# Fourier steps with the real and imaginary halves side by side on 128 rows, fewer index steps, and another written-out order

## The chip, the cores and the metric

The kernel runs on one core of a Trainium2 chip. The metric is the device time of one execution, in microseconds. The core's engines are PE (TensorE, matmuls; PEld is its weight load), DVE (VectorE), ACT (ScalarE), POOL (GpSimd) and SP (SyncE, which here issues nearly all transfers). Each works through its own instructions in order, and they wait for one another by semaphores.

## The reference

Two branches read the same input x of 2,048 positions and 512 channels, and a gate mixes them:

```python
x = A_u
g = _sigmoid((x * gate_w).sum(-1, keepdims=True))
a = _A_ref(x, ...)      # state-space convolution
b = _B_ref(x, ...)      # linear attention, 32 heads of 16
return g * a + (1 - g) * b

# _A_ref: a filter of 2,048 taps for each channel, applied by Fourier transform
P = jnp.exp(logdA[:, :, None] * l[None, None, :])
K = jnp.einsum("dn,dnl,dn->dl", Cc, P, dB).real
Kf = rfft2(pad(K, L));  Uf = rfft2(pad(u, L))
y = irfft2(Uf * Kf)[:, :L] + u * Dskip

# _B_ref: phi = concat(softmax(p), softmax(-p)) for queries and keys
kv = jnp.einsum("bhsf,bhsd->bhfd", phi_k, v);  z = phi_k.sum over s
o = (phi_q @ kv) / (phi_q . z + 1e-6);  return o @ wo
```

## The kernel before, in words

**What is computed where.** The filter is made in 16 units of 32 channels: PE makes arguments (args), ACT takes exponentials (E, line 71) and sines (cs, line 71), DVE multiplies them to tables (A, lines 1012 to 1027, and R, lines 1036 and 1040), and PE multiplies A by R to the taps of the unit (kps, line 175), which are evicted to KD. Both the input and the filter go through a Fourier transform of 4,096 points in two steps. *Stage a* multiplies by the table W1 (line 589 for the input, line 1067 for the filter) and is evicted to XAu or XA; *stage b* (fft_stage_b, line 186) multiplies, for each of 32 residues, by a table TB and is evicted to xst or XK. The input's spectrum goes to DRAM (XUd) and comes back as XUX or XUY. Then DVE multiplies the spectra (t, line 1129), PE does the first inverse step (psz, line 1156), the result Zr goes to DRAM (Zd, line 1167) and comes back turned (ZT, line 1176), PE does the second inverse step (psy, line 1218) on top of the attention's result, DVE multiplies by the gate (ou, line 1240), and the output is written (line 1249). This is done for channels 0 to 127, 128 to 255, 256 to 383, then for units 12 and 13 (64 channels), 14 (32) and 15 (32). Unit 15 is turned on the core itself, without DRAM (pszn, psyn).

**The layout of the two Fourier steps.** Before, the 128 rows between the steps hold two groups of 64 rows for two halves of the channels; real and imaginary parts lie side by side along the row. Stage a of the input is, for a chunk, 8 matmuls of 256 columns with 64 weight columns each; stage a of the filter is 4 matmuls of 256 columns with 128 weight columns. Stage b is, for each residue, four matmuls over 64 rows: real and imaginary part times two row groups, with sine, cosine and negated sine in TB.

**What sets the order.** The program is a list of 1,070 steps. A step has a name and an engine or a choice of two: an eviction may be on ACT or DVE, other table steps on DVE or POOL. Plan.ORDER is a written-out order of all steps, Plan.SIDES the choices of engine, Plan.RINGS the choices between two PSUM pools. run() emits the steps in that order, so each engine, and SP's queue of transfers, gets its own steps in the order of the list and works them off strictly so. In this text a step is called by its name and a number that counts the steps of that name as the program adds them: zw.14 is the fifteenth write of a Zd block.

**Names that the text uses.** *First 74 us:* `first` makes the index columns (build_index_cols, lines 50 to 55); tg1 (line 250) and tg2 (line 251) make the arguments of a trigonometric table and tgs (ACT) its sines; w1 (lines 261 and 263) makes W1; tbn (line 270) the negated table; tjs (line 287) scales a table for the inverse; st1 to st3 (lines 318 to 321) split parameters into two parts, which pzw writes to DRAM (line 325) and pzr reads back; p_t (lines 359, 360), p_cn (line 426), p_dd (its negation is line 435) and others belong to the chain of the parameters, which ends with p_de; ud.0 to ud.3 are the loads of the input (UD, line 1342), four transfers each; xps turns the input for the attention. *Attention:* pk and vp (lines 699, 738) are keys and values, ek and eq exponentials on ACT, kvp their product; z1 to z5 are the norms, aw writes them to DRAM, ar reads them back spread out (ax, line 870) and em multiplies by them (Eq, line 877). *Transfers at the end:* zw (line 1167) and zr (line 1176) write and read Zd, out (line 1249) writes the output.

The step that hands a chunk of stage a to ACT or DVE is an eviction:

```python
def copy(self, o, i):
    if self.cur.at == "ACT":
        self.nc.scalar.copy(out=o, in_=i)
    else:
        self.nc.vector.tensor_copy(out=o, in_=i)
```

## Time and profile before

| what | value |
|---|---|
| median of 3 runs | 306.41 us (304.59 to 309.04) |
| profiled execution: time | 307.27 us |
| profiled execution: span | 305.4 us |
| matmuls / weight loads | 4,732 / 4,758 |
| DVE, ACT, PE, POOL busy | 256.1, 239.2, 219.2, 48.2 us |
| granted TensorE clock, mean | 0.92 |
| moved by transfers | 35.95 MB |

A group line of the profile reads: source line, engine, operation, output tile <- input tiles, shapes, number of instructions | busy us, mean ns of one | idle time of the engine just before, and what ended it. A timeline line reads: start, length, engine, line, operation, shapes, number merged, and in brackets idle time before with what ended it. A line of the chain of waits reads: start, length, what. SPq is SP's queue: the length of a transfer's line there is the time until SP had issued it, not until it landed.

### The profile page before, as it was taken

Reading aid. Unit: us, or ns where it says so; the run is one execution under the profiler, and the core shown is the slowest. Engines: PE = TensorE matmul, PEld = TensorE weight load, DVE = VectorE, ACT = ScalarE, POOL = GpSimd, SP = SyncE. Lnnn points to the kernel's source line nnn. Section 1 sums busy time; section 2 is a strip of 40 time slices with the busy share of each in tenths; the row PEclk is TensorE's granted clock in tenths of the full one; section 3 lists DMA queues with packets and bytes.
Section 4 is the critical chain, followed back from the end, with each engine's and each line's share of the span. In section 5 each row is a group of like instructions: output and inputs, shape, how many; then the busy total and the mean of one; then the engine's idle time right before and its main releaser. Section 6 shows DMA issues by size and latency. Waiting matters only on the chain.

```text
span 305.4 us, 10610 instructions
## 1 busy us (share of the span) xinstructions
PE 219.2 (72%) x4732; PEld 140.7 (46%) x4758; DVE 256.1 (84%) x339; ACT 239.2 (78%) x328; POOL 48.2 (16%) x53
## 2 busy tenths in 40 slices
...
GB/s 151 250 200 83 60 0 2 104 105 82 126 49 161 210 3 54 156 2 119 67 242 20 137 12 172 77 361 149 75 39 81 301 110 147 228 111 108 175 63 113
DMA packets 62620, 35.95 MB, mean 118 GB/s; under 512 B 46192, under 2 KB 56048, under 8 KB 62576
## 3 DMA queue, kind: packets, MB, share of 16 engines
...
q10 hardware_dynamic: 4224, 0.92, 1.9%
...
## 4 chain that ended last, share of the span: by engine, by line
DVE 25%; PE 24%; ACT 18%; DMA 12%; issue 6%; SPq 1%; ACTq 0%; DVEq 0%
DMA ax<-apd 5%; DMA Zd<-Zr 4%; PE pk L699 4%; PE vp L738 4%; PE kps L175 4%; PE psB L186 3%; DVE R L1040 2%; ACT cs L71 2%; ACT E L71 2%; DVE A L1012 2%; ACT XK L142 2%; PE psz L1156 2%; ACT XA L142 2%; DMA ZT<-Zd 2%; DVE Dtab L360 2%
## 5 line engine op out<-in xcount | busy, mean ns | idle before, releaser
L175 PE MATMUL kps<-R,A 128*32 128x64 bf16 x1472 | 26.0, 227 | 12.8 <-issue 6.4
L71 ACT ACTIVATE E<-args 128x1024 bf16<-128x1024 f32 x32 | 32.7, 1058 | 0.1
L175 PEld LDWEIGHTS <-A 128*32 128x32 bf16 x1472 | 24.0, 152 | 17.5 <-issue 9.0
L71 ACT ACTIVATE cs<-args 128x1024 bf16<-128x1024 f32 x32 | 30.6, 1063 | 0.2 <-DVE R L1040 0.2
L186 PEld LDWEIGHTS <-TB 64*128 64x128 bf16 x1024 | 20.9, 98 | 15.3 <-issue 11.9
L589 PE MATMUL psA<-W,UD 128*64 128x256 bf16 x128 | 14.0, 352 | 11.4 <-DVE XAu L144 4.8
L1012 DVE TENSOR_TENSOR A<-Ctab,Dtab 128x2048 bf16<-128x2048 bf16 x16 | 19.6, 1222 | 2.7 <-PE kps L175 2.7
L1036 DVE TENSOR_TENSOR R<-E,cs 128x2048 bf16<-128x2048 bf16 x16 | 19.5, 1220 | 1.3 <-ACT cs L71 1.3
L142 ACT CAST XK<-psB 128x1024 bf16<-128x1024 f32 x15 | 15.5, 1043 | 6.4 <-PE psB L186 5.2
L508 PE MATMUL xps<-ident,UD 128*128 128x128 bf16 x64 | 8.2, 309 | 16.2 <-DMA UD<-in_A_u_dram 9.2
L714 DVE TENSOR_REDUCE Zk<-Ek 128x64 f32<-128x1024 bf16 x16 | 18.7, 1212 | 1.3 <-ACT Ek L71 1.3
L1040 DVE TENSOR_TENSOR R<-E,cs 128x2048 bf16<-128x2048 bf16 x16 | 19.5, 1220 | 0.0
L589 PEld LDWEIGHTS <-UD 128*64 128x64 bf16 x128 | 10.6, 200 | 15.7 <-issue 9.7
L71 ACT ACTIVATE Eq<-pq 128x512 bf16<-128x512 f32 x32 | 17.1, 619 | 0.4 <-PE pq L811 0.4
...
L71 ACT ACTIVATE Ek<-pk 128x512 bf16<-128x512 f32 x32 | 16.8, 604 | 0.6 <-PE pk L699 0.4
L811 PE MATMUL pq<-xT,Wqp 128*128 128x512 bf16 x64 | 17.0, 408 | 0.0
L1156 PE MATMUL psz<-t,TI 128*128 128x512 bf16 x51 | 16.4, 415 | 0.7 <-issue 0.2
L186 PE MATMUL psB<-XAu,TB 64*128 64x128 bf16 x256 | 11.8, 247 | 6.6 <-DVE xst L144 3.2
L142 ACT CAST XA<-psA 128x1024 bf16<-128x1024 f32 x14 | 14.4, 1058 | 2.8 <-PE psA L1067 2.8
L910 PE MATMUL bps<-wo 128*128 128x512 bf16 x58 | 16.2, 380 | 0.5 <-DVE wo L144 0.2
L699 PE MATMUL pk<-WW,xT 128*128 128x512 bf16 x61 | 16.2, 399 | 0.3 <-issue 0.2
...
## 6 DMA issues: line engine op xcount, KB each, us to landing
...
```

Of the source, the lines that this page charges most:

```text
L71: return self.nc.scalar.activation(**kw)
L142: self.nc.scalar.copy(out=o, in_=i)
L175: nc.tensor.matmul(kps[32 * dj:32 * dj + 32, g4, e, :], lhsT=A[:, ka, :, :, d].rearrange("p a b -> p (a b)"), rhs=R[:, kr, d, :], start=(i ...
L186: nc.tensor.matmul(ps[:, e, sl, :], lhsT=fc.TB[rows, r, 1 - ri:3 - ri, :].rearrange("p a b -> p (a b)"), rhs=XA[rows, r, ri, :], start=(ri ...
L589: nc.tensor.matmul(box.ps[64 * e:64 * e + 64, i, :], lhsT=g.UD[:, :, 64 * h + 32 * e + 4 * g4 + i], rhs=W1, start=True, stop=True, tile_po ...
L699: nc.tensor.matmul(box.ps[:], lhsT=xT[:, st, kt, :], rhs=g.WW[:, kt, :], start=(kt == 0), stop=(kt == 3))
L714: nc.vector.tensor_reduce(out=z, in_=e, axis=mybir.AxisListType.X, op=ALU.add)
L811: nc.tensor.matmul(box.ps[:], lhsT=g.Wqp[:, kt, 128 * m:128 * m + 128], rhs=xT[:, 4 * b:4 * b + 4, kt, :], start=(kt == 0), stop=(kt == 3))
L1012: nc.vector.tensor_tensor(out=c.A[:, 0:2].rearrange("p o a b c -> p (o a) b c"), in0=g.C[:, 0:2, :, d0:d0 + 32].rearrange("p o a c -> p (o ...
L1036: nc.vector.tensor_tensor(out=c.R[:, :, :, 32:64], in0=t.E[:].rearrange("p e x t -> p (e x) t")[:, :, 32:64].unsqueeze(1).to_broadcast([12 ...
L1040: nc.vector.tensor_tensor(out=c.R[:, :, :, 0:32], in0=t.E[:].rearrange("p e x t -> p (e x) t")[:, :, 0:32].unsqueeze(1).to_broadcast([128, ...
L1156: nc.tensor.matmul(box.ps[:, nr * hb:nr * hb + nr, :], lhsT=fc.TI[:, k].rearrange("p t h a -> p (t h a)"), rhs=box.t[:, k, rt:rt + nr, :], ...
```

## The change

The rows between the two Fourier steps now hold the real part in rows 0 to 63 and the imaginary part in rows 64 to 127 of the same channels.

- W1 is kept as two halves. Stage a (new function fft_stage_a) does two matmuls of 128 columns for each 64 weight columns, one into the upper and one into the lower rows: 16 per chunk, for the input and for the filter.
- TB holds two tables instead of three, already different in the upper and the lower rows (new step `two` makes their two offsets), so the negated table (tbn, two steps) is not made. Stage b is one matmul over 128 rows for each residue, with all columns: a quarter as many matmuls.
- The channel order within a unit (kgen_chunk) and the access patterns of the evictions XAu, XU, XA and XK follow the new layout. An eviction still moves 1,024 elements of each row.
- build_index_cols makes eight index columns in one tile and casts them with one instruction instead of eight. One iota of 128 is kept and used in w1, sel0 and at0, where four others were made.
- The list has 1,069 steps, and ORDER, SIDES and RINGS are new.

Counted from the list: matmuls of stage a of the input 128 to 256, of the filter 64 to 256; of stage b 1,024 to 256.

Steps by engine, before and after: DVE 263 and 274, ACT 274 and 271, POOL 29 and 20, PE 274 each. From POOL to DVE go three of the ten tg1 (net), the second st1, st2 and st3, one tjs, two p_cn and p_t.14; from DVE to POOL go w1, at3 and p_t.9.

SP's queue, first part. Before: ud.0 wqk ld ud.1 ud.3 ud.2 wv wsm pzw.1 pzw.0 pzr.0 pzr.1. After: wsm wqk ud.1 wv ld ud.0 ud.3 pzw.0 ud.2 pzw.1 pzr.0 pzr.1.

SP's queue, last part. Before: zw.11 xur.7 zr.4 zr.5 zw.12 zw.13 zr.6 zr.7 out.0 zw.14 zr.8 zr.9 out.2 out.1 out.3. After: zw.11 xur.7 zr.4 zr.5 out.0 zw.12 zw.13 zr.6 zr.7 zw.14 zr.8 zr.9 out.1 out.2 out.3. out.0 follows ou.3, and zr.8 and zr.9 read what zw.14 wrote.

PE, last part. Before: psB32.0 psy128.4 psy128.5 kps.8 psz.14 psA.15 psB32.1 psy64.0 pszn.0 psyn32.0 psy32.0. After: psy128.4 psy128.5 psB32.0 kps.8 psA.15 psz.14 psB32.1 psy64.0 pszn.0 psyn32.0 psy32.0. Zr.14 is on DVE before and on ACT, behind XA.15, after.

The first norms. Before, on ACT: z3.0, four cs, z5.0; after: z3.0 eq.7 z5.0, four cs. On DVE, from z4.0 to em.0, before: Rl.0 Rh.1 Rl.1 A1.1 A2.1 A3.1 KD.0 A1.2 A2.2 z2.1; after: A2.0 A3.0 Rh.0 Rl.0 Rh.1 Rl.1.

```diff
 def build_index_cols(nc, pool):
     idx_i = pool.tile([128, 1], I32, name="idx_i")
     nc.gpsimd.iota(idx_i[:], pattern=[[0, 1]], base=0, channel_multiplier=1)
-    cols = {}
-
-    def mk(name, shift, mask):
-        t = pool.tile([128, 1], I32, name=f"ii_{name}")
+    want = (("p", 0, 127), ("p31", 0, 31), ("p63", 0, 63), ("h16", 4, 7), ("h2", 4, 1), ("s5", 5, 3), ("b5", 5, 1), ("b6", 6, 1))
+    t = pool.tile([128, len(want)], I32, name="ii")
+    f = pool.tile([128, len(want)], F32, name="if")
+    for k, (name, shift, mask) in enumerate(want):
         if shift:
-            nc.vector.tensor_scalar(out=t[:], in0=idx_i[:], scalar1=shift, scalar2=mask,
+            nc.vector.tensor_scalar(out=t[:, k:k + 1], in0=idx_i[:], scalar1=shift, scalar2=mask,
                                     op0=ALU.arith_shift_right, op1=ALU.bitwise_and)
         else:
-            nc.vector.tensor_single_scalar(out=t[:], in_=idx_i[:], scalar=mask, op=ALU.bitwise_and)
-        f = pool.tile([128, 1], F32, name=f"if_{name}")
-        nc.vector.tensor_copy(out=f[:], in_=t[:])
-        cols[name] = f[:, 0:1]
-    mk("p", 0, 127); mk("p31", 0, 31); mk("p63", 0, 63)
-    mk("h16", 4, 7); mk("h2", 4, 1); mk("s5", 5, 3); mk("b5", 5, 1); mk("b6", 6, 1)
-    return cols
+            nc.vector.tensor_single_scalar(out=t[:, k:k + 1], in_=idx_i[:], scalar=mask, op=ALU.bitwise_and)
+    nc.vector.tensor_copy(out=f[:], in_=t[:])
+    return {name: f[:, k:k + 1] for k, (name, _, _) in enumerate(want)}
...
-    ORDER = ("01020H0R0a0b0d030V0e000S040M0m0n0c050706080o0T0W191a0U0N0O0Z0X0f15160g0P0h0I111b0B0C0-0J17180K0L340_1c0Q1d1p0i100D091e12"
...
+    ORDER = ("0H1o0R0S0T0a0W0b0c01020405030y0z0A0X070I080B0d0M0J06000Y0K1L0N0C0O0e0p0q1s090P0Z140U0f110D3j3l180r39191a0L0V1O0Q15160-1d"
...
-                    d = 16 * e + 4 * dj + g4
+                    d = 8 * g4 + 4 * e + dj
                     nc.tensor.matmul(kps[32 * dj:32 * dj + 32, g4, e, :], lhsT=A[:, ka, :, :, d].rearrange("p a b -> p (a b)"),
                                      rhs=R[:, kr, d, :], start=(i == 0), stop=(i == len(terms) - 1), tile_position=(0, 32 * dj), skip_group_check=True)
 
 
+def fft_stage_a(nc, fc, ps, lhsT):
+
+    for ri in range(2):
+        nc.tensor.matmul(ps[64 * ri:64 * ri + 64], lhsT=lhsT, rhs=fc.W1[:, ri].rearrange("p r d -> p (r d)"), start=True, stop=True, tile_position=(0, 64 * ri))
+
+
 def fft_stage_b(nc, fc, ps, XA, r0, ns):
 
     for sl in range(ns):
-        r = r0 + sl
-        for ri in range(2):
-            for e in range(2):
-                rows = slice(64 * e, 64 * e + 64)
-                nc.tensor.matmul(ps[:, e, sl, :], lhsT=fc.TB[rows, r, 1 - ri:3 - ri, :].rearrange("p a b -> p (a b)"), rhs=XA[rows, r, ri, :],
-                                 start=(ri == 0), stop=(ri == 1), tile_position=(64 * e, 0), skip_group_check=True)
+        nc.tensor.matmul(ps[:, sl, :], lhsT=fc.TB[:, r0 + sl].rearrange("p a b -> p (a b)"), rhs=XA[:, r0 + sl], start=True, stop=True)
...
-        F.w1 = g.ctmp.tile([128, 32, 2], BF16, name="w1")
+        F.w1 = g.ctmp.tile([128, 2, 32], BF16, name="w1")
...
     def w1(e):
-        c4 = F.one[:, 0:4]
-        iota_f(nc, c4, [[1, 4]])
-        e.tensor_scalar(out=F.one[:, 4:8], in0=c4, scalar1=g.icol["s5"], scalar2=None, op0=ALU.is_equal)
+        e.tensor_scalar(out=F.one[:, 4:8], in0=g.c128[:, 0:4], scalar1=g.icol["s5"], scalar2=None, op0=ALU.is_equal)
         for dj in range(4):
             e.tensor_scalar(out=fc.W1[:, :, :, dj], in0=F.w1[:], scalar1=F.one[:, 4 + dj:5 + dj], scalar2=None, op0=ALU.mult)
     E("w1", w1, r="ic w10 w11", w="W1 one")
+
+    def two(e):
+        e.tensor_scalar(out=F.two[:, 0:1], in0=g.icol["b6"], scalar1=SIN - COS, scalar2=COS, op0=ALU.mult, op1=ALU.add)
+        e.tensor_scalar(out=F.two[:, 1:2], in0=g.icol["b6"], scalar1=COS - MSIN, scalar2=MSIN, op0=ALU.mult, op1=ALU.add)
+    E("two", two, r="ic", w="two")
     tb = lambda i, hf: fc.TB[:, 16 * hf:16 * hf + 16, i, :]
     for hf in range(2):
         c, kc = iot([[2, 16], [128, 64]], 1 + 32 * hf, 1024)
-        for i, o in ((0, SIN), (1, COS)):
-            trig(lambda i=i, hf=hf: tb(i, hf), 1024, p63, lambda o=o: o, c, kc, f"TB{i}{hf}")
-        E("tbn", lambda e, hf=hf: e.tensor_scalar(out=tb(2, hf), in0=tb(0, hf), scalar1=-1.0, scalar2=None, op0=ALU.mult), r=f"TB0{hf}", w=f"TB2{hf}")
+        for i in range(2):
+            trig(lambda i=i, hf=hf: tb(i, hf), 1024, p63, lambda i=i: F.two[:, i:i + 1], c, kc, f"TB{i}{hf}", None, "two ")
...
-                    X.t = g.xau.tile([128, 32, 2, 128], BF16, name="XAu", tag="XAu")
-                box.ps = psum([128, 4, 256], "psA")
-                for i in range(4):
-                    for e in range(2):
-                        nc.tensor.matmul(box.ps[64 * e:64 * e + 64, i, :], lhsT=g.UD[:, :, 64 * h + 32 * e + 4 * g4 + i],
-                                         rhs=W1, start=True, stop=True, tile_position=(0, 64 * e))
+                    X.t = g.xau.tile([128, 32, 4, 64], BF16, name="XAu", tag="XAu")
+                box.ps = psum([128, 8, 128], "psA")
+                for i in range(8):
+                    fft_stage_a(nc, fc, box.ps[:, i, :], g.UD[:, :, 64 * h + 8 * g4 + i])
 
             def ea(g4=g4, box=box, X=X):
-                i = box.ps[:].rearrange("p g (x d) -> p x d g", d=4)
+                i = box.ps[:].rearrange("p c (r d) -> p r d c", d=4)
                 box.ps = None
-                return X.t[:].rearrange("p r i (d g) -> p (r i) d g", d=4)[:, :, :, 4 * g4:4 * g4 + 4], i
+                return X.t[:, :, :, 8 * g4:8 * g4 + 8], i
...
-                box.ps = psum([128, 2, 4, 128], "psB")
-                fft_stage_b(nc, fc, box.ps, X.t, r0, 4)
+                box.ps = psum([128, 4, 256], "psB")
+                fft_stage_b(nc, fc, box.ps, X.t[:].rearrange("p r d c -> p r (d c)"), r0, 4)
                 if r0 == 28:
                     X.t = None
 
             def eb(r0=r0, box=box):
-                i = box.ps[:].rearrange("p e s (d g) -> p s d e g", d=4)
+                i = box.ps[:].rearrange("p s (d c) -> p d s c", d=4)
                 box.ps = None
-                return box.s[:].rearrange("p d s (e g) -> p s d e g", e=2)[:, r0 % 8:r0 % 8 + 4], i
+                return box.s[:, :, r0 % 8:r0 % 8 + 4, :], i
...
-                    XA.t = g.xap[XA.slot].tile([128, 32, 2, XA.nd // 2], BF16, name="XA", tag="XA")
-                box.ps = psum([128, 4, 256], "psA")
-                for i in range(4):
-                    nc.tensor.matmul(box.ps[:, i, :], lhsT=K.KD[:, cc, i, :], rhs=W1, start=True, stop=True)
+                    XA.t = g.xap[XA.slot].tile([128, 32, XA.nd], BF16, name="XA", tag="XA")
+                box.ps = psum([128, 8, 128], "psA")
+                for i in range(8):
+                    fft_stage_a(nc, fc, box.ps[:, i, :], K.KD[:, cc, i // 2, 64 * (i % 2):64 * (i % 2) + 64])
                 if cc == nu - 1:
                     K.KD = None
 
             def ex(cc=cc, box=box):
                 slot = (0 if new else 2) + cc
-                i = box.ps[:].rearrange("p g (x d) -> p x d g", d=4)
+                i = box.ps[:].rearrange("p c (r d) -> p r c d", d=4)
                 box.ps = None
-                return XA.t[:].rearrange("p r i (c d g) -> p (r i) c d g", d=4, g=4)[:, :, slot, :, :], i
+                return XA.t[:, :, 32 * slot:32 * slot + 32].rearrange("p r (c d) -> p r c d", d=4), i
...
-                box.ps = psum([128, 2, ns, ng], "psB")
+                box.ps = psum([128, ns, nd], "psB")
                 fft_stage_b(nc, fc, box.ps, XA.t, r0, ns)
                 if end:
                     XA.t = None
 
             def xk(box=box):
                 box.XK = g.fpool.tile([128, ns, nd], BF16, name="XK", tag="XK", bufs=g.P.k["XK"])
-                o = box.XK[:].rearrange("p s (c e x) -> p (s c) e x", e=2, x=16)
-                i = box.ps[:].rearrange("p e s (c x) -> p (s c) e x", x=16)
+                i = box.ps[:]
                 box.ps = None
-                return o, i
+                return box.XK[:], i
...
-        fc.W1 = persist.tile([128, 32, 2, 4], BF16, name="W1")
-        fc.TB = persist.tile([128, 32, 3, 64], BF16, name="TB")
+        fc.W1 = persist.tile([128, 2, 32, 4], BF16, name="W1")
+        fc.TB = persist.tile([128, 32, 2, 64], BF16, name="TB")
```

67 lines of the change are left out of this document (31 added, 36 removed).

## The prediction

> **What bounds the kernel now.** I read the page's totals first, then the busy time of each engine by stage, then the timeline of the first and the last stage, and the chain of waits where a stage is tight.
>
> ```profile
> span 305.4 us, 10610 instructions
> PE 219.2 (72%) x4732; PEld 140.7 (46%) x4758; DVE 256.1 (84%) x339; ACT 239.2 (78%) x328; POOL 48.2 (16%) x53
> ```
>
> The windows below are start:end, length, then busy time and instructions of PE, PEld, DVE, ACT and POOL, the granted clock, DMA share and GB/s.
>
> ```profile
> 0.00:74.00 74.00, 38.84 (x435) 31.07 (x437) 67.78 (x125) 57.28 (x70) 40.51 (x45) 0.91 0.51 99
> 74.00:113.00 39.00, 37.42 (x667) 19.84 (x673) 33.83 (x39) 34.29 (x64) 7.70 (x9) 1.00 0.44 124
> 113.00:148.00 35.00, 27.00 (x464) 13.41 (x464) 29.70 (x48) 34.35 (x57) 0.00 (x0) 0.90 0.25 79
> 148.00:248.00 100.00, 81.74 (x1871) 52.36 (x1883) 95.80 (x103) 94.09 (x121) 0.00 (x0) 0.98 0.43 131
> 248.00:306.00 58.00, 34.24 (x1305) 24.03 (x1306) 29.00 (x28) 19.23 (x21) 0.00 (x0) 0.78 0.73 137
> ```
>
> No engine bounds the whole. The tables and the parameter chain (to 74 us) are DVE's, 67.78 of 74; the keys (to 113) are PE's, 37.42 of 39; then ACT's (34.35 of 35), then DVE and ACT together; after 248 no engine is full, and the time is that of transfers and of the order in which SP issues them. So I price the change stage by stage.
>
> **The first 74 us.** The change drops seven casts, the two negated tables (tbn) and four iotas, and it moves steps between DVE and POOL.
>
> ```profile
> 1.20 0.15 DVE L53 TENSOR_SCALAR ii_p<-idx_i 128x1 int32<-128x1 int32 x1 [1.20 <-POOL mpi L224]
> ...
> 3.12 0.15 DVE L55 CAST if_b<-ii_b 128x1 f32<-128x1 int32 x1
> ...
> 3.42 0.74 DVE L250 TENSOR_SCALAR tgv<-tgc,if_p 128x1024 int32<-128x1024 f32 x1
> ...
> 9.58 0.99 DVE L261 TENSOR_SCALAR one<-one,if_s 128x4 f32<-128x4 f32 x1
> ...
> 10.68 0.79 DVE L263 TENSOR_SCALAR W<-w,one 128x64 bf16<-128x64 bf16 x4
> ...
> 29.22 1.50 DVE L359 TENSOR_TENSOR pt<-pt,pt 128x512 f32<-128x512 f32 x1
> ...
> 32.54 0.69 DVE L359 TENSOR_TENSOR pt<-pt,pt 128x512 f32<-128x512 f32 x1 [0.23 <-ACT pt L71]
> ...
> 33.15 1.22 DVE L144 CAST XAu<-psA 128x1024 bf16<-128x1024 f32 x1
> ```
>
> ```profile
> 57.21 2.74 POOL L359 TENSOR_TENSOR pb<-pb,pb 128x1024 f32<-128x1024 f32 x1 [20.51 <-DVE pb L409]
> ...
> 57.76 2.89 DVE L435 TENSOR_SCALAR trg<-trg 128x1024 bf16<-128x1024 bf16 x1
> ...
> 70.89 0.43 DVE L435 TENSOR_SCALAR trg<-trg 128x1024 bf16<-128x1024 bf16 x1
> ```
>
> ```profile
> L270 POOL TENSOR_SCALAR TB<-TB 128x1024 bf16<-128x1024 bf16 x2 | 6.3, 3144 | 0.1
> ```
>
> ```profile
> 57.76 2.90 DVE trg L435
> ```
>
> DVE's own tally: the sixteen tiny index steps take 3.27 - 1.20 = 2.07 us; nine of them and two for "two" remain, 11/16 of it, 1.42: -0.65. w1 goes to POOL: -(0.99 + 0.79) = -1.78. Up to the end of the parameter chain the new sides give DVE two 1,024-wide evictions fewer: -2.44; ACT, 57.28 of 74 busy, takes them. Onto DVE come two long tg1 (2 x 0.74), the second st1 to st3 (at most 3 x 0.69), tjs and two p_cn (3 x 0.43, by the like operation at 70.89), and p_t.14 for p_t.9 (a 1,024-wide pass, at most 1.38, for a 512-wide one, 0.69): +5.5. Net +0.7 us.
>
> Against that stands what POOL does to DVE. The same operation took 2.89 us while POOL's 2.74 us pass ran and 0.43 without; another pair is 1.50 against 0.69. Those two rows alone hold 2.46 + 0.81 = 3.3 us, and p_t.14, both p_cn, both tbn (6.3 us of POOL) and a tjs leave POOL. The relief lies between nothing (POOL keeps two p_t and gets w1) and twice the two rows, 6.6; I take 4.7, nearer the upper end, because the chain of waits, whose line for it stands last of the fences on POOL, has the 2.9 us on it. The term: 0.7 - 4.7 = **-4 us, between -6 and +1**. The Trainium skill, SBUF — State Buffer, section on who interferes with whom, says that VectorE in its fast modes and GpSimd hold a shared port pair as an exclusive lock, the loser blocking for the whole instruction; the trace agrees, 2.89 being about POOL's 2.74 and not a little over 0.43. The sum would be the same without that rule.
>
> The negated table itself is read only by stage b of the input, which follows all evictions of stage a; that it goes saves POOL's time and nothing on PE's path.
>
> **Stages a and b on PE.**
>
> ```profile
> 59.20 1.74 PE L660 MATMUL gps<-gw,xT 128*128 128x1 bf16 x64
> ```
>
> ```profile
> 79.08 0.65 PE psA L589 x8
> ...
> 86.52 0.55 PE psB L186 x16
> ...
> 217.28 0.59 PE psB L186 x32
> ...
> 221.34 1.97 PE kps L175 x128
> ...
> 236.63 1.05 PE psA L1067 x8
> ...
> 280.97 1.79 PE psB L186 x128
> ```
>
> Stage a of the input: 8 passes of 256 columns per chunk become 16 of 128, equal streaming, twice the weight loads. Bounds: 0.55, sixteen load-and-pass pairs of 128 columns as psB has them, to 0.65 plus eight pairs at twice the kps pace (1.97/128 = 15 ns for 32 weight columns, 31 for 64) = 0.90. I take 0.65, as streaming is unchanged and eight loads fit in it now. Only the 8 chunks of the keys' stage are on the path: 0, between -0.8 and +2. Stage b of the input: 4 pairs with 256 columns, half of 1.05, against 0.55: nothing. Stage a of the filter: four pairs (0.53) become sixteen (0.55 to 0.90), four chunks of it after 248: +0.4, at most +1.5. Stage b at 128 channels: eight pairs of 128 columns, between 0.53 and 0.59: nothing. At 32 and 64 channels 128 short passes take 1.79; 32 full-height loads with short passes, at the pace of L660 (1.74/64 = 27 ns), take 0.87: -0.9 in each of three blocks after 248, -2.7. The evictions keep their 1,024 elements; I price them alike.
>
> What speaks against stage a: the Trainium skill, TensorEngine Tiling, Gotcha 2, says that column tiling excludes fast weight load, and the filter's stage a now tiles columns. TensorE: Matmul & The Clock Gate, section on LDWEIGHTS, prices a load at columns / 1.2 ns, 53 ns for 64 columns, an estimate of 0.85 us per chunk if loads alone pace it; the sum would then be about 300.3. No run here shows such loads paced alone.
>
> **The middle.**
>
> ```profile
> 127.53 7.44 ACT cs L71 x8
> ...
> 140.37 7.33 DMA ax<-apd
> 147.72 1.23 DVE Eq L877
> ```
>
> Before, z5.0 stands behind the first cs group on ACT, and the ax transfer then keeps DVE waiting. After, z5.0, aw.0 and ar.0 precede the group, so the 7.33 lie beside the 7.44. DVE was idle only 35 - 29.70 = 5.3 us in that window, ACT was full, and the new order puts six passes between z4.0 and em.0 on DVE (A2.0, A3.0 and four R; 7.4 us at the 1.23 of the Eq row), while the ax transfer alone takes 7.33 and its write and issue come before it, so em.0 still waits, with A1.1 and all behind it queued on DVE, and kps.1 on PE behind those. I take **-1 us, between -3 and +3**.
>
> **The end.**
>
> ```profile
> 262.08 4.97 SPq L1176 DMA_DIRECT2D ZT<-Zd  x2
> ...
> 273.27 1.24 SPq L1167 DMA_DIRECT2D Zd<-Zr  x2
> ...
> 279.47 1.23 DVE L144 CAST Zr<-psz 128x1024 bf16<-128x1024 f32 x1 [2.41 <-PE psz L1156]
> ...
> 280.00 4.98 SPq L1249 DMA_DIRECT2D out_dram<-xT  x4
> ...
> 285.03 1.32 SPq L1167 DMA_DIRECT2D Zd<-Zr  x1
> ...
> 293.48 9.02 SPq L1249 DMA_DIRECT2D out_dram<-xT  x10
> ```
>
> The last far block is ready at 279.47 + 1.23 = 280.70, but its write zw.14 leaves at 285.03: SP was issuing out.0 for 4.98 us. Everything after (zr.8, zr.9, psy32, out.3) hangs on it. After the change out.0 is issued behind zr.5, in SP's gap from 267.05 to 273.27, which holds 6.2 us; it is then ahead of zw.12, which waits only if zr.5 comes late. So 4.33 us go. Given back: psz.14 now follows psA.15 on PE and Zr.14 follows XA.15 on ACT; psA is 0.53, and the eviction pushes Zr.14 by up to another 0.7: +1.2. Of the -2.7 and +0.4 of PE I count -1, because DVE's passes before t32.0 (Rh, Rl, A1, A2, A3) and SP's issues are next. The term: -4.33 + 1.2 - 1 = **-4 us, between -7 and -1**. The final out queue, 9.02 us, keeps its length and shifts with zw.14.
>
> **Sum.** -4 + 0 - 1 - 4 = -9 us on the profiled execution, 307.27 (its span and 1.87 around it), which is 0.86 above the median of 306.41. From the median: **297.4 us**. The lower ends add to -6 - 1 - 3 - 7 = -17, the upper to +1 + 2 + 3 - 1 = +5.
>
> **Rivals.**
>
> ```profile
> 8.15 10.10 SPq L1342 DMA_DIRECT2D UD<-in_A_u_dram  x12
> ...
> 24.78 2.72 SPq L325 DMA_DIRECT2D pz<-pt  x4
> ...
> 33.46 2.09 PE L589 MATMUL psA<-W,UD 128*64 128x256 bf16 x16 [2.89 <-ACT xT L142]
> ```
>
> *The input comes late.* All of UD is issued by 18.25 now; in the new order ud.2 stands on SP behind pzw.0, which waits for st3.0. Now the pz writes go at 24.78; behind half of 2.72 and four UD issues (4 x 0.84 = 3.4) the last quarter would be issued at 29.5, and stage a could lose the start's -4 altogether: 301.4. For it: SP issues in order. Against it: the second stage-a chunk ran at 33.46 anyhow, and st3.0 comes earlier with a lighter DVE. Chance 0.17.
>
> *out.0 is only moved.* If zr.5 or ou.3 are late, out.0's 4.98 lands on zw.12 and zw.13, and zw.14 still leaves near 285: the end gives -1, not -4: 300.4 to 302. Chance 0.10.
>
> *Slower: weight loads of stage a stand bare.*
>
> ```profile
> L589 PEld LDWEIGHTS <-UD 128*64 128x64 bf16 x128 | 10.6, 200 | 15.7 <-issue 9.7
> ```
>
> A load is recorded at 200 ns. Sixteen of them end to end are 3.2 us a chunk instead of 0.65, +2.55 on the 12 chunks on the path (8 in the keys' stage, 4 at the end): +31, 328 us. To come out slower by 2% the change must lose 15 us against my sum, 1.26 us a chunk, so the point is 1.9 us a chunk, 119 ns a pair. Against: eight pairs run in 0.65 now, 81 ns each; at that pace sixteen take 1.3, +0.65 x 12 = +7.8, 305, which is still no change. Chance 0.09.
>
> **Chances and range.** 2%, about what a measurement of this kernel can tell from no change, is 6.1 us: below 300.3 or above 312.5. My forecast has 0.60, in its own range of 291 to 303, nine tenths of it below 300.3; the two rivals inside 2% have 0.27, stage a 0.09, and 0.04 is for both savings failing (306). Faster 0.55, no change 0.36, slower 0.09. The range 290 to 307 leaves out the slower rival and about 0.07 below.
>
> **What would show it.** Right: tgv, TJ and trg on DVE near their shorter times; the first cs group after z5.0; the last Zd write leaving within 1 us of its Zr, with out.0 before the two ahead of it; psB blocks at 32 channels under 1 us; the end of the parameter chain near 70 us instead of 74 and of the keys near 109 instead of 113. Wrong: stage-a chunks above 0.9 us; DVE stretched as before beside POOL; psAu waiting for UD; SP holding zw.12 or zw.14 behind out.0; the window 148 to 248 longer than 100 us for the same work.

## The result, and the profile after

The changed kernel takes 296.98 us (median of 4, 295.95 to 302.3) against 306.74 for the kernel before (median of 4, 304.59 to 309.04): a ratio of 0.967, 95% interval 0.958 to 0.976. The prediction was 297.4. Medians and ranges are of all runs, while ratios leave out disturbed ones, among them the first profiled execution after the change (302.3 us) and the profiled one of a_contig (293.15 us). Every line of "after" below is therefore from a later execution of the changed kernel (`after_again`), 297.03 us with a span of 294.5.

The first two lines of its page, and its count of the queue that carries instructions (transfers, MB, share of 16 engines):

```profile
span 294.5 us, 9724 instructions
PE 224.7 (76%) x4310; PEld 147.5 (50%) x4310; DVE 254.7 (86%) x336; ACT 238.4 (81%) x325; POOL 29.8 (10%) x48
...
q8 instruction: 33, 0.54, 0.8%
```

PE is busier than before (224.7 against 219.2 us) with fewer instructions, POOL is much lighter (29.8 against 48.2), DVE and ACT carry the same. So the time did not come from less work on PE, DVE or ACT. To see where it came from I cut both spans at the same events: the first exponential of the keys, the last matmul of kvp, the end of the second gate step ou.1, and the end. The kernel before (start:end, length, then busy us of PE, PEld, DVE, ACT, POOL, granted clock, DMA share, GB/s):

```profile
0.00:74.80 74.80, 39.24 (x438) 31.27 (x441) 68.58 (x126) 58.07 (x71) 41.22 (x46) 0.91 0.51 99
74.80:119.80 45.00, 43.76 (x815) 22.95 (x825) 38.99 (x45) 40.27 (x76) 6.98 (x8) 1.00 0.37 104
119.80:241.10 121.30, 96.83 (x2012) 58.89 (x2021) 112.93 (x136) 115.95 (x157) 0.00 (x0) 0.96 0.40 121
241.10:305.40 64.30, 39.40 (x1488) 27.60 (x1483) 35.61 (x36) 24.95 (x27) 0.00 (x0) 0.81 0.71 141
```

The changed kernel, cut at the same events:

```profile
0.00:70.60 70.60, 41.53 (x413) 33.45 (x415) 64.69 (x118) 59.63 (x72) 29.84 (x48) 0.76 0.55 115
70.60:118.00 47.40, 47.24 (x786) 27.68 (x785) 39.78 (x48) 39.50 (x74) 0.00 (x0) 1.00 0.32 96
118.00:236.10 118.10, 98.41 (x1928) 60.71 (x1928) 113.25 (x136) 115.47 (x155) 0.00 (x0) 0.99 0.42 124
236.10:294.50 58.40, 37.56 (x1188) 25.66 (x1187) 37.00 (x37) 23.80 (x26) 0.00 (x0) 0.83 0.74 146
```

Start -4.2, keys' stage +2.4, middle -3.2, end -5.9: together -10.9. The prediction had -4, 0, -1 and -4. The sum was close, but two of its terms were too small a gain and one hid a loss. In the keys' stage PE is busy 47.24 of 47.40 us: a full PE, and 3.5 us more of it than before.

Next come rows that answer to those shown of before. First, DVE in the start (timeline):

```profile
15.22 0.88 DVE L249 TENSOR_SCALAR tgv<-tgc,one 128x1024 int32<-128x1024 f32 x1 [1.07 <-POOL tgc L39]
...
16.83 0.62 DVE L288 TENSOR_SCALAR TJ<-tj 128x1024 bf16<-128x1024 bf16 x1
...
18.66 0.43 DVE L288 TENSOR_SCALAR TJ<-tj 128x1024 bf16<-128x1024 bf16 x1 [0.62 <-ACT tj L67]
...
32.32 3.95 DVE L394 SCALAR_TENSOR_TENSOR pb<-pt,pt 128x256 f32<-128x256 f32 x8
...
54.49 0.43 DVE L436 TENSOR_SCALAR trg<-trg 128x1024 bf16<-128x1024 bf16 x1
...
66.21 0.43 DVE L436 TENSOR_SCALAR trg<-trg 128x1024 bf16<-128x1024 bf16 x1
```

The negation of trg that had taken 2.89 us now takes 0.43 both times. The chain of the parameters (its last p_de) ends at 68.8 instead of 73.4.

Then PE, in the keys' stage and behind it. The first row is two chunks of the input's stage a, the second one chunk, the third two chunks of the filter's stage a, the last a block of stage b at 32 channels:

```profile
68.84 2.51 PE L178 MATMUL psA<-W,UD 128*64 128x128 bf16 x32 [0.66 <-ACT xst L138]
71.52 1.35 PE L178 MATMUL psA<-W,UD 128*64 128x128 bf16 x16 [0.16 <-DVE XAu L140]
...
252.45 1.08 PE L178 MATMUL psA<-W,KD 128*64 128x128 bf16 x32
...
274.74 0.95 PE L184 MATMUL psB<-XA,TB 128*128 128x32 bf16 x32
```

A chunk of the input costs 1.35 us, 84 ns a pair of load and pass (1.26 where two follow each other); the filter's 0.54, 34 ns a pair. In the same 64-column form they differ by a factor of 2.5. Stage b at 32 channels has gone from 1.79 to 0.95.

Last the end, ACT and SP:

```profile
256.65 5.77 SPq L1240 DMA_DIRECT2D out_dram<-xT  x4
266.17 2.03 SPq L1158 DMA_DIRECT2D Zd<-Zr  x2
...
274.80 1.01 ACT L138 CAST Zr<-psz 128x1024 bf16<-128x1024 f32 x1
...
275.84 0.33 SPq L1158 DMA_DIRECT2D Zd<-Zr  x1
...
282.02 10.08 SPq L1240 DMA_DIRECT2D out_dram<-xT  x10
```

out.0 is issued by 262.42, zw.12 leaves at 266.17 unhindered, and zw.14 leaves 0.03 us after its eviction, where it had waited 4.33.

### The profile page after: what moved, and what is told of

Same layout as the page of the kernel before. It is cut to its first block, busy times and chain, and to the rows that moved or that the text cites. A ratio compares the mean times of both kernels' runs of the same rounds, so it can differ in the third digit from the quotient of the medians.

```text
span 299.6 us, 9699 instructions
## 1 busy us (share of the span) xinstructions
PE 221.8 (74%) x4285; PEld 146.4 (49%) x4310; DVE 255.4 (85%) x336; ACT 238.4 (80%) x325; POOL 29.8 (10%) x48
## 4 chain that ended last, share of the span: by engine, by line
PE 34%; ACT 30%; DVE 13%; DMA 11%; issue 8%; SPq 1%; ACTq 0%; DVEq 0%
ACT cs L67 7%; PE kps L171 5%; PE pk L692 5%; PE vp L731 5%; ACT E L67 5%; PE psA L178 5%; PE psz L1147 4%; PE psB L184 3%; DMA wqk<-in_B_wqkv_dram 3%; ACT L64 3%; ACT Zr L138 3%; DMA ax<-apd 2%; DMA ZT<-Zd 2%; ACT Eq L67 2%; ACT xT L138 2%
## 5 line engine op out<-in xcount | busy, mean ns | idle before, releaser
L171 PE MATMUL kps<-R,A 128*32 128x64 bf16 x1472 | 27.6, 231 | 9.3 <-issue 7.2
L171 PEld LDWEIGHTS <-A 128*32 128x32 bf16 x1472 | 25.7, 160 | 13.3 <-issue 9.6
L178 PE MATMUL psA<-W,UD 128*64 128x128 bf16 x256 | 21.1, 316 | 8.8 <-DVE pt L361 3.8
L178 PEld LDWEIGHTS <-UD 128*64 128x64 bf16 x256 | 20.1, 246 | 11.0 <-issue 10.8
L184 PEld LDWEIGHTS <-TB 128*128 128x128 bf16 x256 | 15.6, 100 | 12.8 <-issue 6.8
L1147 PE MATMUL psz<-t,TI 128*128 128x512 bf16 x52 | 17.0, 430 | 1.8 <-ACT XK L138 0.7
L138 ACT CAST Zr<-psz 128x1024 bf16<-128x1024 f32 x14 | 14.3, 1032 | 3.1 <-PE psz L1147 2.4
L1120 DVE TENSOR_TENSOR t<-XUX,XK 128x1024 bf16<-128x1024 bf16 (+1 forms) x22 | 15.6, 732 | 0.8 <-ACT XK L138 0.8
L731 PE MATMUL vp<-WW,xT 128*128 128x512 bf16 x57 | 15.7, 396 | 0.3
L138 ACT CAST KD<-kps 128x1024 bf16<-128x1024 f32 (+1 forms) x7 | 6.3, 899 | 11.4 <-PE kps L171 11.4
```

The costliest lines, as they stand in the source:

```text
L171: nc.tensor.matmul(kps[32 * dj:32 * dj + 32, g4, e, :], lhsT=A[:, ka, :, :, d].rearrange("p a b -> p (a b)"), rhs=R[:, kr, d, :], start=(i ...
L178: nc.tensor.matmul(ps[64 * ri:64 * ri + 64], lhsT=lhsT, rhs=fc.W1[:, ri].rearrange("p r d -> p (r d)"), start=True, stop=True, tile_positi ...
L184: nc.tensor.matmul(ps[:, sl, :], lhsT=fc.TB[:, r0 + sl].rearrange("p a b -> p (a b)"), rhs=XA[:, r0 + sl], start=True, stop=True)
L731: nc.tensor.matmul(box.ps[:], lhsT=xT[:, st, kt, :], rhs=g.WW[:, 4 + kt, :], start=(kt == 0), stop=(kt == 3))
L1147: nc.tensor.matmul(box.ps[:, nr * hb:nr * hb + nr, :], lhsT=fc.TI[:, k].rearrange("p t h a -> p (t h a)"), rhs=box.t[:, k, rt:rt + nr, :], ...
```

## The experiments

All are compared with the kernel before on the same chip (medians of 305.5 to 306.9 us). The table cuts each profiled execution at the events named above.

| kernel | median us | ratio, 95% interval | start | keys | middle | end |
|---|---|---|---|---|---|---|
| before | 306.7 | | 74.8 | 45.0 | 121.3 | 64.3 |
| after_again | 296.40 | 0.958 to 0.970 | 70.6 | 47.4 | 118.1 | 58.4 |
| order_only | 309.88 | 1.007 to 1.013 | 75.8 | 44.2 | 124.5 | 63.2 |
| layout_only | 301.66 | 0.979 to 0.986 | 73.3 | 48.7 | 118.3 | 59.3 |
| b_out | 302.81 | 0.983 to 0.992 | 74.7 | 45.1 | 120.2 | 62.2 |
| a_outback | 300.23 | 0.976 to 0.989 | 70.4 | 47.4 | 117.8 | 61.1 |
| a_contig | 292.49 | 0.939 to 0.960 | 69.9 | 43.3 | 119.6 | 57.6 |
| a_split_b | 302.25 | 0.980 to 0.989 | 70.2 | 49.1 | 123.4 | 55.5 |
| a_shift | 296.15 | 0.964 to 0.975 | 71.1 | 47.3 | 119.9 | 54.8 |
| a_stride | 295.71 (one run) | | 70.0 | 46.0 | 119.3 | 57.8 |
| a_pool | 303.16 | 0.985 to 0.995 | 79.1 | 43.2 | 120.9 | 58.2 |
| a_z5late | 306.98 | 1.000 to 1.010 | 70.3 | 47.4 | 128.7 | 58.4 |
| a_out1 | 295.05 | 0.959 to 0.970 | 70.6 | 47.4 | 117.3 | 57.6 |

### The two halves of the change, apart

`after_again` is the changed kernel once more.

> The changed kernel again, for a second profile. 295.5 to 298 us by every theory. If stage a of the input is paced by its weight loads (theory A), its chunks take 1.3 to 1.4 us in the keys' stage here too, and the keys' stage ends no earlier than before although the parameter chain ends 4 to 5 us earlier; if the long chunks were a mishap of the first profile (theory B), they take 0.65 here and the keys' stage ends near 109.

`order_only` is the kernel before with the new list:

```diff
-    ORDER, SIDES, RINGS: of the kernel before
+    ORDER, SIDES, RINGS: of the changed kernel, tbn.0 and tbn.1 kept on POOL, each behind the sines that it negates
```

> The old layout and tables (with both negated tables on POOL, and the old index columns) in the new order with the new sides. Theory A (the new layout loses 5 us in the keys' stage through 16 instead of 8 loads per chunk, the order wins all the rest): 291 to 295 us, stage a of the input 0.65 us a chunk. Theory B (the layout carries a gain of its own, in the keys' stage nothing is lost): 298 to 302.

`layout_only` is the changed kernel with the old list:

```diff
-    ORDER, SIDES, RINGS: of the changed kernel
+    ORDER, SIDES, RINGS: of the kernel before, two.0 on DVE behind first.0, tbn left out
```

> The new layout, tables and index columns in the old order with the old sides. Theory A: 306 to 311 us: 5 lost in the keys' stage, 1 to 3 won by the lighter start and the end. Theory B: 299 to 304.

The order alone makes the kernel slower, 309.88; the layout alone gives 5 us, 301.66; together they give 10. So the 291 to 295 that I had expected of the order, and the 306 to 311 of the layout by the same theory, were wrong: the gain was not the order's alone. Theory B missed the order too (298 to 302) and had the layout right (299 to 304).

The start shows why. Neither half shortens it as both do (Dtab ends at 73.9, 72.0 and, with both, 68.8). With the order alone the late trg rows are short (mean 427 ns), yet the chain is late before it begins. POOL and DVE of order_only (timeline):

```profile
8.33 3.23 POOL L270 TENSOR_SCALAR TB<-TB 128x1024 bf16<-128x1024 bf16 x1 [2.21 <-ACT TB L71]
...
15.39 3.19 POOL L270 TENSOR_SCALAR TB<-TB 128x1024 bf16<-128x1024 bf16 x1
...
20.49 0.88 DVE L250 TENSOR_SCALAR tgv<-tgc,one 128x1024 int32<-128x1024 f32 x1 [2.79 <-POOL tgc L39]
```

The two negated tables stand in POOL's queue ahead of the iotas that DVE's last tgv needs: that step starts at 20.49 instead of 15.22, 5.3 us later, and Dtab ends 5.1 us later. The negated table, which I had called nothing on PE's path, is 5 us on DVE's path once DVE is relieved. (The place of tbn in this list was mine; another could cost less.)

From the start of that last tgv to the end of Dtab it takes 57.9 us before, 56.2 in layout_only, 53.4 in order_only and 53.6 after. So the new sides and order shorten DVE's chain by 2.6 to 4.5 us in either layout, and the layout alone by 1.7.

The keys' stage gets its loss with the layout (48.7 and 47.4 against 45.0 and 44.2), in either order. The middle gets its gain with the layout, too: 118.3 and 118.1 with it, 121.3 and 124.5 without.

### What out.0 is worth

`b_out` is the kernel before with one step moved:

```diff
-    SP: ... zr.5 zw.12 zw.13 zr.6 zr.7 out.0 zw.14 zr.8 zr.9
+    SP: ... zr.5 out.0 zw.12 zw.13 zr.6 zr.7 zw.14 zr.8 zr.9
```

> The kernel before with one step moved: out.0 right behind zr.5 on SP, as in the new order. If out.0 in front of zw.14 held the end up by its 4.33 us: 302.4 to 303.5 us, zw.14 leaves within 1 us of its Zr. If out.0 is only moved and holds zw.12 and zw.13 up in turn: 305 to 307.

It takes 302.81, 4 us less, as expected. `a_outback` undoes the same step in the changed kernel:

```diff
-    SP: ... zr.5 out.0 zw.12 zw.13 zr.6 zr.7 zw.14 zr.8 zr.9
+    SP: ... zr.5 zw.12 zw.13 zr.6 zr.7 out.0 zw.14 zr.8 zr.9
```

> The changed kernel with the first out write back behind the eviction zr.7, where it stood before; the rest as changed. Theory A, SP's 4.98 us of issuing stand ahead of the last far write again: it leaves 3 to 4.5 us later behind its eviction, and the kernel takes 299.5 to 301 us, as the kernel before lost 4 us by the same move the other way (302.8 against 306.9). Theory B, with the shorter second step other work ahead of the last far write is what comes last, and SP's place is hidden: 296 to 298 us.

300.23: 3.8 us more, in A's range. zw.14 is less late than I had said, though: it leaves 1.96 us behind its eviction (which ends at 275.58), not 3 to 4.5 (SP of a_outback):

```profile
273.01 4.49 SPq L1240 DMA_DIRECT2D out_dram<-xT  x4
277.54 1.53 SPq L1158 DMA_DIRECT2D Zd<-Zr  x1
282.44 2.13 SPq L1167 DMA_DIRECT2D ZT<-Zd  x2
```

It leaves 1.7 us later than after, the issue itself then takes 1.53 instead of 0.33, and the read behind it leaves 3.2 us later (282.44 against 279.24). So in either layout the turn is worth about 4 us of the median, and about half of it comes after the write has left. That out.0's transfer then shares the DMA engines with zw.14 would explain it; I did not separate the two.

### What stage a of the input costs, and why

`a_contig` takes other weights, side by side:

```diff
-                    fft_stage_a(nc, fc, box.ps[:, i, :], g.UD[:, :, 64 * h + 8 * g4 + i])
+                    fft_stage_a(nc, fc, box.ps[:, i, :], g.UD[:, 8 * g4 + i, 64 * h:64 * h + 64])
```

> The changed kernel with one edit: the input's stage a takes as weights 64 elements that lie side by side (one row of 128 of the input's tile) in place of the 64 of one channel, which lie 256 bytes apart; its input part is therefore the transform of other numbers, and everything behind is unchanged in size and order. Theory A, the distance between the weights sets the time of a load: in the changed kernel a chunk of 16 pairs took 1.30 to 1.40 us with the weights apart, 81 ns a pair, and the filter's, with 32 pairs side by side, 1.08, 34 ns a pair. The chunks then fall to 0.55 to 0.65 us, the keys' stage (first exponential of the keys to last matmul of KV, 47.4 us) shortens to 42 to 45, and the kernel takes 291.5 to 294.5 us. Theory B, the pair costs 81 ns for another reason (the form with 64 columns, the eviction behind it): chunks stay at 1.2 to 1.4 us, and the kernel takes 295.5 to 297.5.

Theory A holds. A single chunk, and two together (PE of a_contig):

```profile
70.87 0.64 PE L178 MATMUL psA<-W,UD 128*64 128x128 bf16 x16 [0.49 <-DVE XAu L140]
...
74.81 1.13 PE L178 MATMUL psA<-W,UD 128*64 128x128 bf16 x32
```

The keys' stage falls from 47.4 to 43.3, the kernel to 292.49 (288.5 to 297.48). The same change in the first half of the input, whose chunks run at 31 to 52 us, moves nothing: Dtab ends at 68.6.

`a_stride` tries eight distances between neighbouring weights:

```diff
+                    k = (128, 64, 32, 16, 8, 4, 2, 1)[g4]
-                    fft_stage_a(nc, fc, box.ps[:, i, :], g.UD[:, :, 64 * h + 8 * g4 + i])
+                    fft_stage_a(nc, fc, box.ps[:, i, :], g.UD[:].rearrange("p t c -> p (t c)")[:, 0:64 * k].rearrange("p (t c) -> p t c", c=k)[:, :, (8 * g4 + i) % k])
```

> The changed kernel with the weights of the input's stage a taken at another distance in each of the eight chunks of a half: 256, 128, 64, 32, 16, 8, 4 and 2 bytes from one of the 64 weights to the next, in this order; the input part is therefore the transform of other numbers. Known: 256 bytes costs 81 ns a pair (1.30 us a chunk), 2 bytes about 34 ns (0.55 us); the filter's loads of 32 weights 64 bytes apart run at 15 ns a matmul. Theory A, the cost goes with the distance down to about the pace of the matmuls: 128 bytes 0.75 to 1.0 us a chunk, 64 bytes and less 0.55 to 0.70. Theory B, every distance but side by side costs the same: seven chunks of 1.2 to 1.4 and one of 0.55. By A a second tile of the input with 32 or 64 channels to a row would give the gain of the kernel with weights side by side without another layout of the chip's memory; by B only a copy would. The kernel's time lies between 290.5 and 296.5 us either way.

PE of a_stride, from a distance of 16 bytes (first row) and 8 bytes (second row) in the first half; then, in the second half, from 256 bytes, 128 and 64 bytes together, 32 bytes, and 4 and 2 bytes together:

```profile
42.46 1.18 PE L178 MATMUL psA<-W,UD 128*64 128x128 bf16 x16
44.73 0.71 PE L178 MATMUL psA<-W,UD 128*64 128x128 bf16 x16
...
68.26 1.34 PE L178 MATMUL psA<-W,UD 128*64 128x128 bf16 x16 [1.35 <-ACT xst L138]
69.82 2.30 PE L178 MATMUL psA<-W,UD 128*64 128x128 bf16 x32 [0.22 <-DVE xst L140]
...
75.16 1.18 PE L178 MATMUL psA<-W,UD 128*64 128x128 bf16 x16
...
80.68 1.09 PE L178 MATMUL psA<-W,UD 128*64 128x128 bf16 x32
```

Neither theory: there is one step, between 16 bytes (1.18) and 8 (0.71). From 16 to 256 bytes a chunk costs about 1.15 to 1.34; at 8 bytes it costs 0.71 and at 4 and 2 bytes 0.55, close to the 0.55 to 0.64 of side by side. The Trainium skill, SBUF — State Buffer, in a note in the section on the DMA port swizzle, says that SBUF is read in lines of 16 bytes and that a read needs at least two hits in a line to run at full pace; the trace agrees, with the step at just that place: at 16 bytes each weight has a line to itself, at 8 bytes two share one. Had I weighed that rule in the prediction, the term of the keys' stage could have had the right sign.

These are prices at a granted clock of 1.00 (the chunk at 64 bytes alone ran at 0.62). From 50 to 52 us the granted clock was 0.50, and there a chunk took 1.07 side by side (PE of a_contig, first row) and 1.40 at 256 bytes (after, second row):

```profile
50.40 1.07 PE L178 MATMUL psA<-W,UD 128*64 128x128 bf16 x16 [2.25 <-ACT XAu L138]
...
50.59 1.40 PE L178 MATMUL psA<-W,UD 128*64 128x128 bf16 x16 [1.58 <-ACT XAu L138]
```

The chunk with the weights apart takes nearly the same at either clock (1.35 and 1.40), the one side by side does not (0.64 and 1.07). So the distance costs 0.71 us a chunk at the full clock and 0.33 at half.

`a_pool` gives the second half of the input weights side by side, each channel its own, by copies on POOL behind p_t.10, an engine that is otherwise idle after 44 us:

```diff
+        for k in range(8):
+            nc.gpsimd.tensor_copy(out=g.UE[:, 8 * k:8 * k + 8, :], in_=g.UD[:, :, 64 + 8 * k:72 + 8 * k].rearrange("p t c -> p c t"))
...
-                    fft_stage_a(nc, fc, box.ps[:, i, :], g.UD[:, :, 64 * h + 8 * g4 + i])
+                    fft_stage_a(nc, fc, box.ps[:, i, :], g.UE[:, 8 * g4 + i, :] if h else g.UD[:, :, 8 * g4 + i])
```

> The changed kernel, in which GpSimd copies the second half of the input (64 of its 128 channels a row) into a tile with each channel's 64 elements side by side, in eight copies behind its last step of the parameter chain, where it was at work on tables that are wanted late; stage a of the second half takes its weights from that tile. The output is the reference's. Theory A: a copy of 512 elements takes 0.8 to 1.5 us (the copy gwr of 512 took 0.78), all end before 47 us, the eight chunks at 68 to 83 us fall from 1.35 to 0.55 to 0.65, DVE's chain keeps its end at 68.8 to 70, and the kernel takes 291 to 294 us, most of what the kernel with wrong weights gave. Theory B: DVE's short forms wait for GpSimd's copies as they did in the kernel before (trg 2.89 us beside GpSimd, 0.43 alone), the parameter chain ends at 71 to 74, and what is gained in the keys' stage is lost ahead of it: 295 to 299 us.

The keys' stage gains 4.2 us (43.2), and the start loses 8.5 (79.1): theory B, and worse than its range, 303.16. POOL and DVE of a_pool:

```profile
33.38 9.57 POOL L388 COPY UE<-UD 128x512 bf16<-128x512 bf16 x8
...
32.30 9.71 DVE L399 SCALAR_TENSOR_TENSOR pb<-pt,pt 128x256 f32<-128x256 f32 x8
```

The same eight passes of DVE took 3.95 us after (32.32, above). They end at 42.01, the copies at 42.95: DVE did not get past POOL while it copied. That is 5.8 us; the rest comes behind it, as POOL's tables, which follow the copies, now run until 53 us beside more of DVE: two of its passes there take 2.30 and 2.02 us (46.05 and 48.39) that took 0.69 and 0.44 after. This is the contention that the start's term was built on, shown from the other side: 9.57 us of copies on POOL beside a full DVE cost the start 8.5. (The row behind theory A's price, gwr, is a copy of 128 elements, not of 512; a copy of 512 took 1.2 us.) The Trainium skill, SBUF — State Buffer, section on who interferes with whom, names this case beside the fast modes: a VectorE step with two inputs in SBUF contends with a GpSimd step that reads SBUF; the trace agrees, as these passes have two inputs.

### What stage b is worth, and what stops PE

`a_split_b` cuts each matmul of stage b in two of half the columns, with the same weights loaded for each:

```diff
-        nc.tensor.matmul(ps[:, sl, :], lhsT=fc.TB[:, r0 + sl].rearrange("p a b -> p (a b)"), rhs=XA[:, r0 + sl], start=True, stop=True)
+        n = ps.shape[2] // 2
+        for k in range(2):
+            nc.tensor.matmul(ps[:, sl, n * k:n * k + n], lhsT=fc.TB[:, r0 + sl].rearrange("p a b -> p (a b)"), rhs=XA[:, r0 + sl, n * k:n * k + n], start=True, stop=True)
```

> The changed kernel with every matmul of the second Fourier step cut into two of half the columns, with the same weights loaded for each: the same work and order, but as many instructions more as the change took away. Theory A, the halved count of stage b is what lets the new order pay: the blocks at 32 channels go from 0.95 to 1.5 to 1.8 us, the stretch from the last eviction of b to the second out group (32.3 us in the changed kernel, 39.4 with the old layout in the new order) goes to 36 to 39, the last stretch by 2 to 4, and the kernel takes 303 to 308 us. Theory B, the order's gain does not hang on it (the old layout in the new order lost by its index steps on GpSimd): 296 to 299.5 us.

302.25: 5 to 6 us over the changed kernel, between the ranges of A (303 to 308) and B (296 to 299.5). It puts back less than I had said: 256 of the 768 matmuls that stage b had lost, with their loads 512 instructions (10,236 against 9,724). The block at 32 channels (PE of a_split_b) is as A had it:

```profile
271.32 1.77 PE L186 MATMUL psB<-XA,TB 128*128 128x16 bf16 x64
```

But the last stage did not become longer, as A had said it would: it is shorter (55.5 against 58.4), perhaps because the stall of 3.95 us that the changed kernel has there (below) is missing; the longest of its kind in this run is 1.8. The loss is all in the middle, 123.4 against 118.1. There the stretch from the last eviction of b to ou.1 is 32.3 us after, 38.2 with stage b cut, and 39.4 with the old layout in the new order. Groups of PE in the window from 204 to 245 us show what differs (busy us, mean ns | idle before, and what ended it). The changed kernel:

```profile
L171 PE MATMUL kps<-R,A 128*32 128x64 bf16 x640 | 11.4, 228 | 0.6 <-ACT Zr L138 0.6
```

Stage b cut:

```profile
L171 PE MATMUL kps<-R,A 128*32 128x64 bf16 x544 | 10.2, 232 | 3.1 <-issue 2.7 <-ACT Zr L138 0.3
...
L939 PE MATMUL args<-selE,statC 64*128 64x512 bf16 x8 | 2.0, 436 | 1.8 <-issue 1.8
```

The old layout in the new order:

```profile
L175 PE MATMUL kps<-R,A 128*32 128x64 bf16 x576 | 10.1, 225 | 5.5 <-issue 5.1 <-ACT Zr L142 0.3
```

"issue" is time in which PE waited for nothing that the profile shows, in the midst of a group of matmuls. With more matmuls ahead of it the new order meets 4.5 and 5.1 us of it there; with few, none. The old order is another matter: the same stretch takes 38.2 us before and 37.1 in layout_only, with 1.4 us of such idle and none, so most of what the layout gains in the old order's middle lies elsewhere. And the kernel before has a long stall of this kind in its last stage, too, as long as the changed kernel's:

```profile
267.86 0.75 PE L175 MATMUL kps<-R,A 128*32 128x64 bf16 x35 [3.90 <-issue]
```

`a_shift` asks what it is, by 128 more instructions of PE at 62 us:

```diff
-        for st in range(16):
+        for st in 2 * list(range(16)):
             for kt in range(4):
                 nc.tensor.matmul(G.ps[:, st:st + 1], lhsT=xT[:, st, kt, :], rhs=g.gw[:, kt:kt + 1], start=(kt == 0), stop=(kt == 3))
```

> The changed kernel with the 64 small matmuls of the gate's sum written twice (about 128 instructions of TensorE more at 62 us, 1.7 us on an engine that waits there). Theory A, the stalls without a releaser inside one group of matmuls are TensorE waiting for its own instructions, which come in transfers of 16 KB, 256 instructions: half a transfer more ahead moves every boundary by 128 instructions, so the stall of 3.94 us in the filter's matmuls at 258.9 us shrinks under 1.5 us or stands at another matmul, others appear elsewhere, and the kernel takes 293 to 300 us. Theory B, that stall belongs to the work at that place (its operands, a bank): it stays at the same matmul of the same group with 3.5 to 4.2 us, and the kernel takes 296 to 298.5.

Theory A. The group of 128 matmuls with the long stall, after:

```profile
256.83 2.10 PE L171 MATMUL kps<-R,A 128*32 128x64 bf16 x117
262.87 0.40 PE L171 MATMUL kps<-R,A 128*32 128x64 bf16 x11 [3.95 <-issue]
```

and in a_shift:

```profile
256.84 1.05 PE L171 MATMUL kps<-R,A 128*32 128x64 bf16 x53
259.27 1.41 PE L171 MATMUL kps<-R,A 128*32 128x64 bf16 x75 [1.38 <-issue]
```

The stall has moved from behind the 117th matmul to behind the 53rd: 64 matmuls with their 64 loads earlier, which is exactly the 128 instructions that were put in (9,852 against 9,724). It belongs to a place in the stream of instructions, not to the work. The queue that carries instructions moved 0.54 MB in 33 transfers, 16 KB each; the trace has one of them from 259.85 to 261.32, within the stall of 258.93 to 262.87. In a_shift one ran from 256.83 to 257.81, just before the stall, and another from 220.81 to 222.28, before a new stall of 1.4 us at 222.35. In all three PE went on 1.46 to 1.55 us after the transfer's end. So PE was waiting for its own instructions. The total hardly changed (296.15): the stall shrank by 2.6 us, others appeared, and all idle put down to "issue" on PE adds up to 7.7 us after and 7.6 in a_shift. The stages move with the stalls: the middle is 1.8 us longer in a_shift, the end 3.6 shorter.

### The turn in the middle

`a_z5late` puts z5.0 and the transfers behind it back behind the cs group:

```diff
-    ACT: z3.0 eq.7 z5.0, four cs        SP: aw.0 ar.0 ar.1 behind z5.0
+    ACT: z3.0 eq.7, four cs, z5.0       SP: aw.0 ar.0 ar.1 behind z5.0
```

> The changed kernel with the queries' first sum z5.0 and the transfers behind it (a write and its two reads) moved back behind the first group of cs, where they stood before: the one visible turn in the middle undone. Theory A, the turn is worth little, as the middle is bound by DVE and ACT, which are busy over 95% of it either way: z5.0 ends near 137 in place of 127 us, the first em leaves 6 to 9 us later, but the last matmul of KV to the second out group goes from 118.1 to 118.5 to 120.5, and the kernel takes 296 to 299 us. Theory B, the turn feeds PE and ACT early and is most of the middle's gain of 3: the stretch goes to 121 or more, and the kernel takes 299 to 302 us.

Both theories missed: 306.98, and 10.6 us are in the middle. DVE of a_z5late:

```profile
144.03 1.23 DVE L870 TENSOR_TENSOR Eq<-Eq,ax 128x2048 bf16<-128x2048 bf16 x1 [10.00 <-DMA ax<-apd]
```

DVE stands still for 10 us for ax. After the change the same step waits 1.13 us, as z5.0 and its write go ahead of the cs group. In the kernel before ten other steps of DVE stand ahead of em.0 there; the new order has only six, and all else queues behind em.0. So this is not what the turn gained. The kernel before fills the wait: em.0 waits 0.65 us for ax there, and all eight em together 3.3:

```profile
L877 DVE TENSOR_TENSOR Eq<-Eq,ax 128x2048 bf16<-128x2048 bf16 x8 | 9.8, 1224 | 3.3 <-DMA ax<-apd 3.3
```

layout_only has the old place of z5.0 and the same steps to fill the wait, and its middle is as short (118.3). A list of this kind holds together, and one step put back in it is no measure of that step.

### One more turn at the end

`a_out1` moves out.1 ahead of zr.8. As it ran, all four issues of out.1 went to SP in the gap, and it was half of out.2 that went to ACT:

```diff
-    SP: zw.14 zr.8 zr.9 out.1 out.2 out.3
+    SP: zw.14 out.1 zr.8 zr.9 out.2 out.3
...
-                    (nc.scalar if last and c % 2 else nc.sync).dma_start(out=ov[c], in_=xT[32 * c:32 * c + 32, :, Q - pair:Q + 1, lo:off + nd].rearrange("p j a d -> p j (a d)"))
+                    (nc.scalar if (last or nd == 64) and c % 2 else nc.sync).dma_start(out=ov[c], in_=xT[32 * c:32 * c + 32, :, Q - pair:Q + 1, lo:off + nd].rearrange("p j a d -> p j (a d)"))
```

> The changed kernel with the same kind of turn once more: the second out write goes ahead of the last far reads zr.8 and zr.9, into the 3 us in which SP waits for the last far write to land, with half of its four issues on ACT's queue, which is idle from 275.8 to 282.0. In the changed kernel SP issues ten out transfers from 282.02 to 292.1, 1 us each, while the last eviction's data are there at 288.3. Theory A, the end is SP's queue: six issues are left behind zr.9, the last two leave at 288.4 as their data come, and the span ends 1.5 to 2.5 us earlier, 293.8 to 295.2 us. Theory B, the issues ahead of zr.8 hold it up, or its transfer shares the DMA engines with out: the last read lands 1 to 2 us later, and the kernel takes 296 to 298 us.

The span is 1.5 us shorter, 293.0; from the last gate step to the end it takes 4.3 us instead of 6.2. The median is 295.05 (293.58 to 297.95) against 296.40 (293.9 to 297.34), and the intervals of the two ratios are nearly the same. Of the kernels that leave nothing out it is the shortest, but its lead on the changed kernel is not established.

## Why the prediction was right or wrong

**The start, -4: right, measured -4.2, for the reason given.** trg at 0.43, TJ at 0.62 and 0.43, the parameter chain at 68.8 where I had said near 70. DVE's busy time in the stage fell by 3.9 us (68.58 to 64.69) although it took over steps, and the new sides shorten its chain in either layout. What the term lacked is that the two halves need each other: the sides relieve DVE, and only without the negated tables is POOL in time with its iotas (order_only). The sentence that the negated table saves nothing on a path was true of PE only.

**Stages a and b on PE, 0: wrong, measured +2.4 in the keys' stage.** The step that failed is "I take 0.65, as streaming is unchanged and eight loads fit in it now", with bounds of 0.55 and 0.90. A chunk takes 1.35. Eight loads fitted in 0.65 because they set it: 81 ns a pair then, 84 now, so twice the loads are twice the time. The rival on bare weight loads had this pace and the 1.3 us; I had given it 0.09 and priced it at +7.8 for 12 chunks. Its mechanism holds for the 8 chunks of the input. It does not for the four of the filter, whose weights lie side by side (0.54). Before, the eight chunks took 0.72 each there:

```profile
79.01 0.72 PE L589 MATMUL psA<-W,UD 128*64 128x256 bf16 x8
```

They took 5.8 us together and take 10.4 now, 4.6 more. The stage rose by less: PE's busy time in it by 3.5 us, as 0.7 us fewer of args fall into it (1.0 instead of 1.7), and its idle time fell by 1.1 (1.24 to 0.16), which leaves 2.4. The new order by itself makes the stage 0.8 shorter (order_only). The upper bound came from kps, which has weights 64 bytes apart in loads of 32 columns, scaled to 64 columns, 31 ns; a_stride shows that this does not carry over (64 columns at that distance took 1.18 us for 16 pairs, 74 ns each). The estimate from the Trainium skill, TensorE: Matmul & The Clock Gate, section on LDWEIGHTS, 0.85, was too low for the input and too high for the filter: it has no distance in it. The rule on column tiling (the Trainium skill, TensorEngine Tiling, Gotcha 2) did not decide either: the filter's stage a tiles columns, at 34 ns a pair.

The rest of that part was about right: the filter's stage a 0.54 (0.55 to 0.90 expected), stage b at 32 channels 0.95 (0.87 expected).

**The middle, -1: size and cause wrong, measured -3.2.** I had put it on z5.0 ahead of the cs group, and had read the 7.33 us of the ax transfer as DVE's wait; DVE waited 0.65 us of it ahead of em.0. layout_only has the same middle without the turn. The gain comes with the layout; a_split_b, which undoes a part of stage b's saving, loses 5.3 us there. I had priced stage b at 128 channels at nothing, because a block takes the same time, and had not asked what fewer instructions do for an engine that must also be fed with them. How much of the 5.3 is PE's longer work and how much the stalls is not separated: PE's busy time in the middle rose by 3.0 us (101.45 against 98.41), at a granted clock of 0.94 against 0.99, and the stalls are 4.5. Of the gain itself one stall of the kernel before, 1.37 us, is gone; the cause of the rest stays open.

**The end, -4: right in cause, too small, measured -5.9.** out.0 gave its 4 in the median (b_out, a_outback). The term of stage b, "of the -2.7 and +0.4 of PE I count -1", was too careful: layout_only, with out.0 in its old place, has an end that is 5.0 us shorter than before. The two do not add up, since both shorten the way to zw.14; b_out's end is 2.1 shorter, and both together 5.9. The +1.2 given back did not show: psA.15 and XA.15 ended (273.64 and 274.69) just as psz.14 and Zr.14 could begin, at 273.68, 0.06 us after psz.14's input, and at 274.80, 0.08 us after psz.14. The long stall is in the last stage of both kernels (3.90 and 3.95 us) and no part of the gain.

**The rivals.** *The input comes late* did not happen: SP of the changed kernel issues ud.2 at 22.52 to 24.67, not 29.5, as st3.0 came early, and the first chunk at 31.74 waited for DVE, not for UD. *out.0 is only moved* did not happen: zw.12 left 3.75 us after out.0 was issued. *Weight loads bare* held in kind, not at 200 ns a load but at the 81 ns a pair for which it had itself named no change, and was outweighed.

So 297.4 against 296.98 is partly luck: +2.4 not foreseen in one stage was met by -2.2 and -1.9 in two others.
